# A fused attention and MLP kernel: another order of calls from the second batch on, and 27 scaled copies on VectorE in place of ScalarE

## The chip, the cores and the metric

The kernel runs on one core of a Trainium2 chip. The core has five engines that run their own instruction queues side by side: TensorE (PE in the profile; its weight loads are listed apart as PEld), VectorE (DVE), ScalarE (ACT), GpSimd (POOL) and SyncE (SP), and 16 DMA engines. The metric is the device time of one execution in microseconds; the median of three runs is taken.

## The reference

```python
def _attn_ref(q, k, v, g_q, g_k):          # (8, 12, 448, 64), float32
    def rmsnorm(x, g):
        return x / np.sqrt(np.mean(x * x, axis=-1, keepdims=True) + 1e-06) * g
    q_n, k_n = rmsnorm(q, g_q), rmsnorm(k, g_k)
    scores = 1.0 / np.sqrt(64) * np.matmul(q_n, k_n.transpose(0, 1, 3, 2))
    attn = np.exp(scores - np.max(scores, axis=-1, keepdims=True))
    attn = attn / (np.sum(attn, axis=-1, keepdims=True) + 1e-09)
    return np.matmul(attn, v)

# x: the attention's output as (3584, 768); w_in (768, 2048), w_out (2048, 768), alpha (2048,)
def _moe_ref(x, w_in, w_out, alpha):
    h = x @ w_in
    g = np.maximum(h, 0.0) + alpha * np.minimum(h, 0.0)
    return g @ w_out
```

Attention of 8 batches with 12 heads each, then an MLP with a PReLU between its two products over all 3584 tokens.

## The kernel before

The work of a batch is cut into three groups of four heads; a group has the number y = 3 x batch + i (i = 0, 1, 2), so y runs from 0 to 23. For a group, load_qk fetches q and k (SP's queue), square (L365, GpSimd) and reduce (L386, VectorE) and fold (L403, L406, VectorE) sum the squares, root (L416, L417, ScalarE) takes the inverse root, scale (L423, GpSimd) multiplies, flip or turn (L531, VectorE; or PE with a copy) transposes, and weigh (L541, ScalarE) puts the gains on k. score(y, j) (L588, PE) makes one of seven blocks of scores into a pair of PSUM banks, and soft(y, j) (L602, ScalarE) its exponentials. den and den_pre (L613, L637) sum them on PE, log and invert (L661, L671, ScalarE) make the reciprocal, attend (L613, PE) multiplies with v, and times (L709, VectorE) divides into xT, the MLP's input.

The MLP of a batch b runs over 16 blocks of 128 hidden columns. up(b, ft) (L726, PE, six matmuls of 128x128 by 448 columns) makes h in one PSUM bank, slope(b, ft) writes alpha x h to gT (L766 on ScalarE, L761 on VectorE), and larger(b, ft) (L772, VectorE) takes the larger of h and that; after larger the bank is free for PE. The second product is taken in tiles of 128 tokens by 384 columns: the first as down (L792, PE) with down_end (L803, VectorE, and a store on SP's queue, L778), and from tile 6 on by pairs of tiles with seven products in place of eight: mix_weights, mix_two and mix_rest (L822, L842, L843, L850, mostly GpSimd) form sums of weights and of gT, qa1 to qc2 (L854, PE) multiply them, and qa1v to qc2v (VectorE) add up and send. quad does a whole pair at the end.

PSUM has three pools: "sc", two pairs of banks for scores; "acc", one pair, for attend, den and whatever has its argument spare set to 1; and "mm", two banks for up, down, the q-products, den_pre and the second half of attend. A tile of a pool can be written again when the last reader of the tile that had its place is done. Other pools: q and k as loaded (nat) four places, scaled q and k (qs) three, results (osb) five.

The order of everything is written out by hand as a text, PLAN, of some 1330 calls, such as `up(5,8,1) qa1(14,0) soft(18,5)`. The loop at the end of the kernel makes the calls in that order; each call puts its instructions on the queues of its engines, so the text sets the order on each engine, and an engine never goes past an instruction that waits. Semaphores between engines follow from the tiles.

Of the kernel before, what the change touches and what calls it, by code (L numbers as in the profile page):

```python
# [24 lines left out]
opening() part_square(q,0:1,0:7,act) part_square(q,1:2,0:7,act) part_reduce(q,0:1,0:7) spin(2,0)  # L25
part_reduce(q,1:2,0:7) part_root(q,0:7) part_square(k,0:2,0:3,act) part_scale(q,0:7,7,pool)
part_reduce(k,0:2,0:3) part_square(k,0:2,3:7,act) square(1,q) load_w_in(1) spin(1)
part_reduce(k,0:2,3:7) part_root(k,3:7) reduce(1,q) square(1,k) part_root(k,0:3) gains()
part_turn(q,r0-7) load_qk(3) spin(1,0) part_scale(k,0:3,3,vec) part_turn(k,r0-3)
part_scale(k,3:7,4,vec) part_copy(q,0:7,vec) part_turn(k,r3-7) load_v(0) reduce(1,k) follow(0,k)  # L30
square(2,q) part_copy(k,0:3,vec) part_copy(k,3:7,vec) root(1) square(2,k) score(0,0,0) soft(0,0)
reduce(2,q,0) score(0,4,1) load_w_in(0) score(0,3,0) spin(1) reduce(2,q,1) soft(0,3) score(0,1,0)
scale(1,k) scale(1,q) soft(0,4) score(0,2,0) soft(0,2) reduce(2,k) score(0,6,1) turn_one(1,q)
soft(0,1) turn_one(1,k) score(1,0,1) score(1,3,0) spin(1) score(1,2,0) soft(0,6) root(2) soft(1,0)
load_qk(4) soft(1,3) scale(2,k) scale(2,q) follow(2,q) square(3,q) square(3,k) load_w_in(2)
soft(1,2) score(0,5,1) score(1,1,0) soft(0,5) soft(1,1) score(1,5,0) turn(2) soft(1,5) score(1,6,1)
# [9 lines left out]
slope(0,2) slope(0,3) larger(0,4) up(0,5,0) larger(0,2) larger(0,3) root(5) soft(3,6) slope(0,5)  # L46
soft(3,2) larger(0,5) up(0,6,0) scale(4,k) turn(4) scale(5,q) up(0,8,0) score(4,0,0) slope(0,6)
score(4,1,1) square(6,k) larger(0,6) slope(0,8) score(3,5,0) up(0,9,0) load_w_out(1) scale(5,k)
soft(4,0) square(7,q) larger(0,8) up(0,11,0) load_qk(8) score(4,2,0) score(3,3,0) soft(3,5)
load_v(1) square(7,k) up(0,7,1) soft(4,1) slope(0,9) up(0,10,0) reduce(6,q) square(8,q) reduce(6,k)  # L50
load_w_out(2) soft(4,2) up(0,12,0) slope(0,11) larger(0,9) soft(3,3) score(3,4,0) slope(0,10)
score(4,3,0) larger(0,11) larger(0,10) slope(0,7) larger(0,7) up(0,13,0) soft(3,4) slope(0,12)
larger(0,12) turn(5) up(0,14,0) square(8,k) soft(4,3) score(4,6,0) slope(0,13) score(4,4,1) root(6)
slope(0,14) larger(0,13) up(0,15,0) scale(6,q) reduce(8,q) soft(4,4) score(5,4,0) larger(0,14)
scale(6,k) score(5,0,1) reduce(7,q) slope(0,15) larger(0,15) down(1,0,0) score(5,2,1) score(4,5,0)
soft(4,6) soft(5,0) soft(5,4) soft(5,2) score(5,1,0) soft(4,5) down(0,0,0) turn(6) load_w_out(3)
den(3+4,1) reduce(7,k) attend(3+4,0,0) score(5,5,0) score(5,6,0) soft(5,1) mix_weights(0,1) log(3+4)
invert(3+4) soft(5,5) soft(5,6) mix_weights(0,3) attend(3+4,1,0) score(6,0,1) score(5,3,0) soft(6,0)
score(6,4,0) down_end(0,0) down(2,0,0) soft(5,3) root(7) scale(7,q) load_qk(9) soft(6,4) scale(7,k)
den(5,0) attend(5,0,1) down_end(1,0) mix_weights(0,2) times(3+4,0,0) times(3+4,1,0) times(3+4,1,1)  # L60
load_qk(10) log(5) down(0,1,0) reduce(8,k) invert(5) down_end(2,0) times(5,0,1) times(5,0,0)
times(5,0,3) times(5,0,2) score(6,5,1) mix_weights(0,0) score(6,1,0) down_end(0,1) score(6,6,0)
soft(6,5) turn(7) up(1,1,1) square(9,q) down(1,1,0) root(8) reduce(9,q) soft(6,6) score(6,3,1)
score(7,0,0) slope(1,1) score(6,2,0) up(1,2,0) up(1,0,0) soft(6,1) soft(7,0) soft(6,3) square(9,k)
up(1,3,1) up(1,4,0) slope(1,2) slope(1,0) larger(1,1) down_end(1,1) reduce(9,k) root(9) larger(1,2)
load_qk(11) larger(1,0) slope(1,3) scale(8,q) soft(6,2) up(1,7,0) slope(1,4) larger(1,3) larger(1,4)
scale(8,k) score(7,4,0) slope(1,7) larger(1,7) up(1,5,1) scale(9,q) turn(8) score(7,5,0) soft(7,4)
score(7,1,0) up(1,6,0) square(10,q) slope(1,5) larger(1,5) up(1,10,0) soft(7,5) soft(7,1) up(1,8,1)
scale(9,k) up(1,9,0) reduce(10,q) score(7,2,0) slope(1,6) slope(1,10) larger(1,6) mix_weights(1,1)
score(7,6,0) slope(1,8) slope(1,9) soft(7,6) up(1,12,1) up(1,11,0) soft(7,2) square(10,k) up(1,13,0)  # L70
larger(1,8) larger(1,10) slope(1,12) score(7,3,0) larger(1,9) up(1,14,1) slope(1,11) slope(1,13)
mix_weights(1,3) reduce(10,k) up(1,15,0) load_v(2) soft(7,3) larger(1,12) load_qk(12) score(8,3,0)
score(8,0,0) den(6+7,0) slope(1,14) fold(10) root(10) slope(1,15) soft(8,0) down(2,1,0) larger(1,11)
larger(1,13) square(11,q) log(6+7) score(8,1,0) score(8,4,0) soft(8,3) flip(9,k) scale(10,q)
larger(1,14) larger(1,15) score(8,5,1) mix_weights(3,1) down_end(2,1) reduce(11,q) square(11,k)
weigh(9) soft(8,5) down(3,0,0) soft(8,1) scale(10,k) score(8,2,0) flip(9,q) reduce(11,k)
score(8,6,0) soft(8,4) fold(11) load_qk(13) attend(6+7,0,0) attend(6+7,1,0) score(9,1,0)
score(9,0,0) down_end(3,0) soft(8,2) invert(6+7) score(9,2,1) down(3,1,0) times(6+7,0,0) soft(8,6)
root(11) times(6+7,1,0) load_qk(14) flip(10,q) down(4,0,1) mix_weights(1,2) soft(9,0) times(6+7,1,1)
score(9,5,0) square(12,q) soft(9,1) soft(9,2) scale(11,q) score(9,3,0) square(12,k) reduce(12,q)  # L80
down_end(3,1) soft(9,5) mix_weights(3,2) flip(10,k) scale(11,k) down_end(4,0) den_pre(8)
reduce(12,k) soft(9,3) attend(8,0,0) log_pre(8) score(9,6,0) fold(12) invert(8) root(12)
score(9,4,0) weigh(10) times(8,0,3) down(5,1,0) soft(9,4) times(8,0,1) times(8,0,0) flip(11,q)
down(4,1,0) score(10,0,0) soft(9,6) score(10,3,1) down_end(5,1) times(8,0,2) soft(10,0) soft(10,3)
score(10,2,0) up(2,0,0) up(2,1,0) slope(2,0) score(10,6,0) score(10,1,1) up(2,7,0) up(2,2,0)
down_end(4,1) up(2,4,1) slope(2,1) flip(11,k) soft(10,2) soft(10,1) slope(2,7) up(2,3,0)
mix_weights(2,0) slope(2,2) larger(2,0) scale(12,q) soft(10,6) slope(2,4) up(2,6,0) scale(12,k)
up(2,8,1) larger(2,1) slope(2,3) mix_weights(2,3) mix_weights(1,0) larger(2,7) square(13,k)
larger(2,2) up(2,10,0) square(13,q) up(2,5,0) larger(2,4) weigh(11) up(2,12,1) larger(2,3)
slope(2,6) up(2,14,0) slope(2,8) reduce(13,q) score(10,5,0) slope(2,10) mix_weights(2,2) load_v(3)  # L90
slope(2,5) slope(2,12) slope(2,14) score(10,4,0) soft(10,4) square(14,q) up(2,9,1) up(2,13,0)
soft(10,5) slope(2,13) larger(2,6) larger(2,8) larger(2,10) reduce(13,k) up(2,11,0) larger(2,5)
larger(2,12) load_qk(15) score(11,0,0) fold(13) den(9+10,1) slope(2,11) mix_weights(3,3) qa1(6,0)
up(2,15,0) qa2(6,1) root(13) mix_weights(3,0) flip(12,q) slope(2,9) larger(2,14) larger(2,13)
down(5,0,0) log(9+10) slope(2,15) larger(2,11) larger(2,9) invert(9+10) soft(11,0) square(14,k)
flip(12,k) reduce(14,q) weigh(12) qa1v(6) larger(2,15) mix_weights(2,1) scale(13,q) score(11,3,1)
scale(13,k) score(11,4,0) attend(9+10,0,1) mix_two(6,pool) soft(11,4) qa2v(6) mix_rest(6)
# [1000 lines left out]
```

## Time and profile before

| | us |
|---|---|
| median of three runs | 412.58 (412.21 to 413.02) |
| the profiled execution | 410.69 |
| its span, first to last instruction | 408.6 |
| busy in the span: PE | 395.3 |
| busy in the span: POOL | 299.9 |
| busy in the span: ACT | 270.4 |
| busy in the span: DVE | 268.3 |

A profile line of a group names the line of the code, the engine, the operation, what is written from what, how often, and after the bar the busy time, the mean of one in ns, and the idle time of the engine just before with what ended it. A timeline line has the start, the length, the engine, the line, the operation, the count of instructions drawn together, and in brackets the idle time before and who ended it. The ends of matmuls are modelled, so the length of a group of matmuls overlaps the next one's; starts are the better measure of pace.

### The profile page before, as it was taken

To read this page: it belongs to the slowest core of one execution; us is meant where nothing else is said; L and a number is where in the kernel's file an instruction comes from. 1 tells how busy PE (TensorE), PEld (TensorE's weight loads), DVE (VectorE), ACT (ScalarE), POOL (GpSimd) and SP (SyncE) were. 2 spreads that over 40 slices of the span, in tenths; PEclk is the share of its full clock that TensorE was granted. 3 is DMA by queue.
4 is the path that set the end of the run, shared out by engine and by line. 5 is a ranking of instruction groups with operands and counts; after the bars stand their busy time and mean duration, and the time that the engine had idled before them with its cause. 6 is when DMAs were issued, how large, how long until landed. Compare 5 with 4: busy or idle time off the path is not lost.

```text
span 408.6 us, 11992 instructions
## 1 busy us (share of the span) xinstructions
PE 395.3 (97%) x5083; PEld 210.3 (51%) x5083; DVE 268.3 (66%) x480; ACT 270.4 (66%) x405; POOL 299.9 (73%) x200
## 2 busy tenths in 40 slices
PE   7688999999999999999999999999999999999996
PEld 3344445555455445554455455555555455655664
DVE  3957874676766685779678678886668545654422
ACT  5597686757885876767886987686876874245110
POOL 7977998497796998997796995589496809600780
PEclk9999999999999999999999999999999999999999
DMA  7999699796776794579952595794516000230143
GB/s 260 242 280 227 110 265 165 173 239 177 125 180 154 173 203 108 119 172 185 232 130 83 136 240 145 147 217 102 140 38 131 21 2 22 59 79 0 39 98 98
DMA packets 37222, 58.39 MB, mean 143 GB/s; under 512 B 4769, under 2 KB 28977, under 8 KB 37169
## 3 DMA queue, kind: packets, MB, share of 16 engines
q1 hardware_dynamic: 23232, 45.43, 43.2%
q0 software_dynamic: 13536, 11.81, 19.1%
q8 instruction: 39, 0.64, 0.7%
q10 hardware_dynamic: 400, 0.39, 0.3%
q14 instruction: 15, 0.11, 0.1%
HBM read 58.40 MB, written 11.01 MB: 170 GB/s over the span
## 4 chain that ended last, share of the span: by engine, by line
PE 88%; DVE 4%; DMA 3%; POOL 3%; issue 1%; POOLq 0%; DVEq 0%
PE hT L726 25%; PE hTa L726 9%; PE sc L588 8%; PE op L792 7%; PE qx L854 5%; PE av L613 5%; PE qz L854 4%; PE qc L854 4%; PE oq L854 4%; PE qxa L854 3%; PE avb L613 2%; PE dn L613 2%; PE oqm L854 2%; DMA w_in_sb<-in_moe_w_in_dram 2%; POOL nat L376 2%; DMA arena<-in_g_k_dram 2%
## 5 line engine op out<-in xcount | busy, mean ns | idle before, releaser
L602 ACT ACTIVATE expT<-sc 128x896 f16<-128x896 f32 x168 | 146.3, 916 | 40.9 <-PE sc L588 39.2
L726 PE MATMUL hT<-xT,w_in_sb 128*128 128x448 f16 x558 | 115.9, 353 | 1.6 <-DVE xT L709 1.4
L726 PEld LDWEIGHTS <-w_in_sb 128*128 128x128 f16 x768 | 73.0, 98 | 74.5 <-issue 9.9
L423 POOL TENSOR_TENSOR qs<-nat,rr 128x896 f16<-128x896 f32 x30 | 65.7, 2221 | 26.5 <-ACT rr L417 23.4
L766 ACT ACTIVATE gT<-hT,cols 128x448 f16<-128x448 f32 x92 | 58.4, 636 | 40.0 <-PE hT L726 38.9
L772 DVE TENSOR_TENSOR gT<-hT,gT 128x448 f16<-128x448 f32 x93 | 57.3, 619 | 38.2 <-ACT gT L766 37.5
L365 POOL TENSOR_TENSOR nat<-nat 128x896 f32<-128x896 f32 x30 | 50.7, 1697 | 8.1 <-DMA nat<-in_q_dram 7.7
L588 PE MATMUL sc<-qT,kT 64*32 64x448 f16 (+1 forms) x1092 | 49.4, 355 | 4.3 <-ACT expT L602 1.7
L854 PEld LDWEIGHTS <-gT 128*128 128x128 f16 x352 | 33.4, 98 | 25.5 <-issue 4.1
L726 PE MATMUL hTa<-xT,w_in_sb 128*128 128x448 f16 x198 | 42.9, 353 | 0.0
L842 POOL TENSOR_TENSOR gs<-gT 128x1024 f16<-128x1024 f16 x4 | 8.5, 2127 | 36.7 <-DVE gT L772 36.7
L709 DVE TENSOR_TENSOR xT<-av,rden 64x448 f16<-64x448 f32 (+1 forms) x37 | 27.2, 736 | 10.7 <-ACT rden L671 4.6
L386 DVE TENSOR_REDUCE sp<-nat 128x28 f32<-128x896 f32 x30 | 32.1, 1070 | 2.1 <-POOL nat L365 2.0
L588 PEld LDWEIGHTS <-kT 64*32 64x32 f16 (+1 forms) x1092 | 16.7, 93 | 32.4 <-issue 23.0
L792 PE MATMUL op<-w_out_sb,gT 128*128 128x384 f16 x176 | 30.3, 326 | 0.2 <-DVE xT L709 0.2
L766 ACT ACTIVATE gT<-hTa,cols 128x448 f16<-128x448 f32 x33 | 21.0, 636 | 10.5 <-PE hTa L726 10.0
L772 DVE TENSOR_TENSOR gT<-hTa,gT 128x448 f16<-128x448 f32 x33 | 20.4, 618 | 10.6 <-ACT gT L766 10.2
L613 PEld LDWEIGHTS <-vt 64*32 64x32 f16 x1344 | 19.7, 92 | 12.2 <-issue 1.9
L792 PEld LDWEIGHTS <-gT 128*128 128x128 f16 x192 | 18.3, 98 | 14.5 <-issue 3.0
L613 PE MATMUL av<-expT,vt 64*32 64x448 f16 x896 | 24.3, 350 | 0.0
L850 POOL TENSOR_TENSOR gT<-gT 128x1024 f16<-128x1024 f16 x11 | 23.5, 2133 | 0.0
L854 PEld LDWEIGHTS <-arena 128*128 128x128 f16 x136 | 12.6, 98 | 10.5 <-issue 2.3
(151 smaller groups left out, 572.5 us busy)
## 6 DMA issues: line engine op xcount, KB each, us to landing
nat<-in_q_dram SPq DMA_DIRECT2D x60, 216.0 KB, 4.1
nat<-in_k_dram SPq DMA_DIRECT2D x60, 216.0 KB, 5.0
out_dram<-osb SPq DMA_DIRECT2D x107, 96.0 KB, 3.1
vt<-in_v_dram POOLq DMA_DIRECT2D x8, 672.0 KB, 7.8
w_in_sb<-in_moe_w_in_dram POOLq DMA_DIRECT2D x24, 128.0 KB, 7.3
w_out_sb<-in_moe_w_out_dram POOLq DMA_DIRECT2D x4, 768.0 KB, 8.6
nat<-in_k_dram SPq DMA_DIRECT2D x6, 448.0 KB, 7.8
nat<-in_q_dram SPq DMA_DIRECT2D x5, 448.0 KB, 6.7
```

Source lines behind the costliest of these rows:

```text
L365: nc.gpsimd.tensor_mul(out=sqs[y, nm], in0=t[:, :, :HD], in1=t[:, :, :HD])
L386: nc.vector.tensor_reduce(out=parts[y][:, ts("qk".index(nm), 4 * J), :1], in_=sqs[y, nm], axis=AXIS_X, op=ALU.add,)
L423: nc.gpsimd.tensor_mul(out=t.rearrange("p j d n -> p n j d"), in0=nat[y, nm][:, :, :HD].rearrange("p (n j) d -> p n j d", j=J), in1=r.unsq ...
L588: nc.tensor.matmul(out=sc[ds(64 * g + m * c, m), par, :S].rearrange("p (j c) -> p j c", j=J), lhsT=kT[ds(64 * par, 64), j, g, ts(c, m)], r ...
L602: nc.scalar.activation(out=expT[y][:, j], in_=scs[y, j][:, :, :S], func=AF.Exp, scale=QK_SCALE, bias=EXP_BIAS,)
L613: nc.tensor.matmul(out=accs[g][ds(32 * n, 32), :S], lhsT=weights(g, y, par, c, j), rhs=expT[y][ds(64 * g, 64), j, par, :], start=(j == 0), ...
L709: nc.vector.tensor_mul(out=o, in0=p, in1=q)
L726: nc.tensor.matmul(out=hT[:, :S], lhsT=w_in_sb[:, block_of(g, i), ts(ft, 128)], rhs=xT[b][:, g, i, :], start=(i == 0 and g == 0), stop=(i ...
L766: nc.scalar.activation(out=g, in_=hT[:, :S], func=AF.Copy, scale=alpha_sb[:, ft : ft + 1])
L772: nc.vector.tensor_max(out=g, in0=hT[:, :S], in1=g)
L792: nc.tensor.matmul(out=op[:, :OH], lhsT=gT[:, ft, ts(tile % J, 128)], rhs=w_out_sb[:, ft, ts(oh, OH)], start=(ft == 0), stop=(ft == NF - 1),)
L854: nc.tensor.matmul(out=bank[:, c], lhsT=g[:, ft], rhs=v[:, ft, c], start=(first and ft == 0), stop=(ft == HF - 1), skip_group_check=True,)
```

## The change

The text PLAN is the same, call by call and engine by engine, up to `scale(8,q)`; from there on its calls come in another order, in nearly every line to the end. 27 more calls of slope are marked vec, which puts them on VectorE: (1; 4, 6, 7, 10, 13), (2; 0, 2, 4, 11), (3; 0, 7, 12), (4; 5, 9, 10, 12, 14), (5; 0, 2, 6, 7, 9), (6; 15) and (7; 1, 6, 8, 13), batch first. Which work takes a bank of "acc" changes in a number of calls. The number of instructions of PE (10149 with weight loads and others), POOL (205) and SP (250) stays; ACT has 412 to 385 and DVE 482 to 509.

```diff
-    def slope(b, ft):
+    def slope(b, ft, eng=None):
         hT, g = raised[b, ft]
-        if b == 0 and ft in (2, 3, NF - 4):
+        if eng is nc.vector:
             nc.vector.tensor_scalar(
                 out=g, in0=hT[:, :S], scalar1=alpha_sb[:, ft : ft + 1], scalar2=None,
                 op0=ALU.mult,
             )
         else:
             nc.scalar.activation(
                 out=g, in_=hT[:, :S], func=AF.Copy, scale=alpha_sb[:, ft : ft + 1]
             )
...
-    def load_w_in(c):
+    def load_w_in(c, lo, hi):
...
-    def square(y, nm):
+    def square(y, nm, eng=None, n=1):
...
     def soft(y, j):
-        if j == 0:
+        if y not in expT:
...
-        spin(2)
-        spin(17, False)
+    def factors():
```

load_w_in now takes which of its pieces to load, square which engine and in how many parts, and factors holds the last lines of opening; in the new text they are called so that the instructions of the first part are the same ones in the same order.

Of the text, the places that are spoken of below, in the order of the calls (before, then after). The calls from up(4,0) to the up after up(4,9):

```
up(4,0,0) root(18) larger(4,4) slope(4,7) up(4,3,1) up(4,5,0) score(16,6,0) soft(16,4) scale(17,k)
up(4,6,0) soft(16,1) soft(16,5) flip(17,q) slope(4,0) slope(4,3) larger(4,1) slope(4,5) soft(16,6)
larger(4,7) slope(4,6) mix_two(12,pool) larger(4,0) up(4,8,1) up(4,9,0) flip(17,k) scale(18,q)
weigh(17) slope(4,8) up(4,11,0)
```

```
up(4,0,0) up(4,3,1) soft(16,4) qc1v(10) soft(16,1) larger(4,2) slope(4,0) scale(17,q) soft(16,5)
up(4,5,0) mix_two(12,pool) larger(4,4) scale(17,k) up(4,6,0) flip(17,k) larger(4,1) flip(17,q)
slope(4,3) larger(4,7) larger(4,0) weigh(17) load_qk(20) up(4,8,1) up(4,9,0) scale(18,k) up(4,11,0)
larger(4,3) slope(4,5,vec) slope(4,6) slope(4,8) score(16,6,1) score(17,4,0) larger(4,5)
square(19,q) larger(4,6) soft(16,6) square(19,k) reduce(19,q) den(15+16,1) larger(4,8) scale(18,q)
slope(4,9,vec) reduce(19,k) score(17,5,1) larger(4,9) flip(18,k) slope(4,11) soft(17,5) larger(4,11)
up(4,10,0)
```

The calls from up(5,2) on:

```
up(5,2,0) weigh(19) score(18,4,0) slope(5,1) qc1v(12) score(18,5,1) load_qk(22) score(19,0,0)
up(5,5,0) larger(5,0) reduce(21,q) slope(5,3) larger(5,1) slope(5,2) larger(5,3) up(5,7,1) up(5,4,0)
up(5,6,0) up(5,8,1) qa1(14,0) soft(18,5) reduce(21,k) qa2(14,0) larger(5,2) soft(19,0) slope(5,5)
slope(5,7) slope(5,4) mix_two(14,pool) fold(21) up(5,9,0) root(21) larger(5,5) up(5,11,0)
score(19,2,0) larger(5,7) slope(5,6) larger(5,4) slope(5,8) score(19,1,1) larger(5,6) soft(18,4)
square(22,q) slope(5,9) flip(20,k) score(19,6,0) qa3(14,0) larger(5,8) slope(5,11) soft(19,6)
weigh(20) qa1v(14) mix_rest(14) flip(20,q) qa2v(14) larger(5,9) qb1(14,0) soft(19,2) up(5,13,0)
```

```
up(5,2,0) score(18,4,0) slope(5,0,vec) score(19,0,0) larger(5,0) soft(18,6) load_v(6) score(18,5,1)
slope(5,3) up(5,5,0) larger(5,1) up(5,7,1) up(5,4,0) up(5,6,0) up(5,8,1) qa1(14,0) soft(18,5)
square(21,k) score(19,6,0) score(19,1,1) slope(5,5) larger(5,3) score(19,2,0) qa2(14,0)
slope(5,2,vec) load_qk(22) larger(5,2) mix_two(14,pool) soft(18,4) slope(5,4) reduce(21,k) up(5,9,0)
fold(21) larger(5,5) scale(20,k) up(5,11,0) slope(5,7,vec) up(5,13,1) soft(19,0) larger(5,7)
slope(5,8) root(21) qa3(14,0) mix_rest(14) up(5,10,0)
```

The calls behind attend of heads 15 and 16:

```
attend(15+16,0,1) attend(15+16,1,0) slope(4,13) larger(4,8) larger(4,9) larger(4,11) log(15+16)
reduce(19,k) invert(15+16) larger(4,10) larger(4,12) fold(19) score(17,2,1) score(17,3,0) qa1v(12)
score(17,1,0) larger(4,13) root(19) qa2v(12) reduce(20,q) up(4,15,0) qa3v(12) weigh(18) soft(17,5)
soft(17,2) soft(17,3) flip(18,q) times(15+16,0,0) qb1(12,1) times(15+16,1,0) scale(19,q) slope(4,15)
square(20,k) soft(17,1) up(4,14,0)
```

```
attend(15+16,0,1) slope(4,13) reduce(20,q) soft(17,4) score(17,6,1) larger(4,13) scale(19,k)
qa1v(12) qa2v(12) soft(17,3) flip(18,q) reduce(20,k) qa3v(12) scale(19,q) score(18,0,0) qb1(12,0)
times(15+16,1,1) score(17,2,1) score(17,0,0) soft(17,1) fold(20) score(18,1,0) times(15+16,0,0)
times(15+16,1,0) qb1v(12) flip(19,q) flip(19,k) soft(17,6) soft(18,0) up(4,14,0)
```

More of the change, by code (lines that the diff above doesn't have):

```diff
@@ L24 @@
 PLAN = """
[L25 to L36, printed above, removed]
@@ L45 @@
 larger(0,0) score(3,2,0) score(3,6,0) slope(0,1) load_qk(7) follow(2,k) larger(0,1) slope(0,4)
[L46 to L97, printed above, removed]
@@ new lines @@
+down_end(2,0) times(5,0,1) times(5,0,0) times(5,0,3) times(5,0,2) score(6,5,1) mix_weights(0,0)
+score(6,1,0) down_end(0,1) score(6,6,0) soft(6,5) turn(7) up(1,1,1) square(9,q) down(1,1,0) root(8)
+reduce(9,q) soft(6,6) score(6,3,1) score(7,0,0) slope(1,1) score(6,2,0) up(1,2,0) up(1,0,0)
+soft(6,1) soft(7,0) soft(6,3) square(9,k) up(1,3,1) up(1,4,0) slope(1,2) slope(1,0) larger(1,1)
+down_end(1,1) reduce(9,k) root(9) larger(1,2) load_qk(11) larger(1,0) slope(1,3) scale(8,q)
+scale(8,k) score(7,4,0) up(1,7,0) larger(1,3) mix_weights(1,3) scale(9,k) slope(1,4,vec)
@@ new lines @@
+scale(13,q) larger(2,13) invert(9+10) reduce(14,q) fold(14) score(11,1,0) mix_two(6,pool) qa2v(6)
+attend(9+10,0,0) attend(9+10,1,0) down_end(5,0) score(11,2,0) soft(11,1) score(12,0,0) qa3(6,1)
+times(9+10,0,0) soft(11,0) qb1(6,0) soft(12,0) score(11,6,1) times(9+10,1,1) soft(11,2)
+score(11,5,0) score(12,1,0) mix_rest(6) root(14) qb2(6,0) qc1(6,1) times(9+10,1,0) qa3v(6)
+score(12,3,0) qb1v(6) soft(11,6) flip(13,k) soft(11,5) qb2v(6) soft(12,1) den_pre(11) attend(11,0,1)
+soft(12,3) qc1v(6) square(15,q) log_pre(11) score(12,6,0) invert(11) mix_two(8,pool) score(12,2,1)
@@ new lines @@
+load_qk(16) soft(12,2) qa1(8,0) qa2(8,1) times(11,0,3) weigh(13) flip(13,q) times(11,0,0) soft(12,6)
+qc2(6,0) qa3(8,0) qa1v(8) reduce(15,q) scale(14,q) times(11,0,1) score(13,0,0) times(11,0,2)
+score(12,5,1) qa2v(8) scale(14,k) score(13,6,0) mix_rest(8) qc2v(6) soft(12,5) qa3v(8) up(3,0,0)
+qb1(8,0) score(12,4,0) slope(3,0,vec) square(15,k) load_qk(17) score(13,3,0) soft(13,6) qb2(8,1)
+qb1v(8) larger(3,0) reduce(15,k) up(3,2,0) soft(13,0) soft(12,4) up(3,4,0) qb2v(8) up(3,1,1)
+fold(15) soft(13,3) square(16,q) slope(3,2) up(3,8,0) up(3,3,0) up(3,5,1) score(13,2,0) slope(3,4)
@@ new lines @@
+root(21) qa3(14,0) mix_rest(14) up(5,10,0) score(19,4,0) larger(5,4) score(19,3,0) soft(19,1)
+score(19,5,1) square(22,k) slope(5,6,vec) qb1(14,0) larger(5,6) larger(5,8) qa1v(14) soft(19,6)
+scale(21,k) load_qk(23) soft(19,2) qb2(14,0) flip(20,q) square(22,q) up(5,14,1) qa2v(14)
+slope(5,9,vec) slope(5,11) up(5,15,0) scale(21,q) slope(5,13) slope(5,10) larger(5,9) reduce(22,k)
+larger(5,11) qa3v(14) soft(19,5) larger(5,13) flip(20,k) soft(19,4) up(5,12,0) weigh(20)
+larger(5,10) reduce(22,q) soft(19,3) slope(5,14) fold(22) qb1v(14) slope(5,15) qb2v(14)
@@ new lines @@
+soft(22,4) den(21+22,1) slope(6,13) attend(21+22,0,1) larger(6,10) larger(6,12) slope(6,14)
+score(23,2,0) mix_rest(18) score(23,5,1) soft(23,0) qb1(18,0) qa2(18,1) qa3(18,0) qa1v(18)
+log(21+22) qa1(20,1) score(23,3,0) soft(23,5) larger(6,13) larger(6,14) slope(6,15,vec) larger(6,15)
+invert(21+22) attend(21+22,1,0) qa2v(18) score(23,1,0) mix_two(20,pool,nat) soft(23,2) score(23,4,0)
+mix_rest(20) times(21+22,0,0) qa3v(18) soft(23,3) qb1v(18) mix_two(22,pool,expT) qb2(18,1) qa2(20,0)
+qa1v(20) times(21+22,1,0) score(23,6,0) soft(23,4) times(21+22,1,1) soft(23,1) soft(23,6)
@@ L1034 @@
     acts = dict(
+        factors=factors,
         attend=attend, begin=begin, den=den, den_pre=den_pre, down=down, down_end=down_end,
```

273 lines of the change are left out of this document (156 added, 117 removed).

## The prediction

> **What bounds the kernel now.** I read the busy shares of the page first, then the stretches of the span, then PE's own timeline in places. The page:
>
> ```profile
> span 408.6 us, 11992 instructions
> ...
> PE 395.3 (97%) x5083; PEld 210.3 (51%) x5083; DVE 268.3 (66%) x480; ACT 270.4 (66%) x405; POOL 299.9 (73%) x200
> ...
> L602 ACT ACTIVATE expT<-sc 128x896 f16<-128x896 f32 x168 | 146.3, 916 | 40.9 <-PE sc L588 39.2
> ...
> L766 ACT ACTIVATE gT<-hT,cols 128x448 f16<-128x448 f32 x92 | 58.4, 636 | 40.0 <-PE hT L726 38.9
> L772 DVE TENSOR_TENSOR gT<-hT,gT 128x448 f16<-128x448 f32 x93 | 57.3, 619 | 38.2 <-ACT gT L766 37.5
> ```
>
> PE is busy for 97% of the span. ScalarE and VectorE, between which the change moves work, are busy for 66% each. The stretches (a row: start and length, then busy us and count of PE, PEld, DVE, ACT and POOL, then the granted clock, DMA share, GB/s) say where PE's 3% are:
>
> ```profile
> 97.00:226.00 129.00, 128.82 (x1846) 67.90 (x1844) 93.59 (x177) 96.03 (x141) 109.72 (x62) 1.00 0.70 159
> 226.00:310.00 84.00, 83.82 (x1212) 44.50 (x1205) 61.11 (x117) 65.65 (x96) 66.13 (x37) 1.00 0.62 140
> 310.00:377.00 67.00, 67.00 (x725) 35.64 (x723) 37.77 (x68) 35.73 (x54) 28.30 (x14) 1.00 0.21 46
> 377.00:408.60 31.60, 27.74 (x186) 17.54 (x184) 10.37 (x20) 3.92 (x8) 16.86 (x8) 1.00 0.30 76
> ```
>
> The two orders of calls are the same up to the call scale(8,q), which in the trace lies at about 97 us; nothing before that can change. From 97 to 377 us PE shows 0.18 + 0.18 + 0.00 = 0.36 us without work, and after 377 us it works 27.74 us without a hole, then the last copies and stores follow. So the kernel is bound by the sum of PE's work, and a different order can win only these 0.36 us, what the order itself costs PE, and stalls hidden in the modelled ends of matmuls.
>
> **What the order itself costs PE.** PE's own timeline from 148 us:
>
> ```profile
> 148.16 1.30 PE L726 MATMUL hTa<-xT,w_in_sb 128*128 128x448 f16 x6
> 149.30 1.30 PE L726 MATMUL hT<-xT,w_in_sb 128*128 128x448 f16 x6
> 150.52 0.57 PE L588 MATMUL sc<-qT,kT 64*32 64x448 f16 x16
> 151.03 1.31 PE L726 MATMUL hTa<-xT,w_in_sb 128*128 128x448 f16 x6
> 152.18 2.43 PE L726 MATMUL hT<-xT,w_in_sb 128*128 128x448 f16 x12
> 154.54 0.38 PE L588 MATMUL sc<-qT,kT 64*32 64x448 f16 x8
> 154.74 1.51 PE L613 MATMUL dn<-expT,ones 64*32 64x448 f16 x56
> ```
>
> From start to start an up that an up follows takes 149.30 - 148.16 = 1.14 us, one that a score follows 150.52 - 149.30 = 1.22. A score followed by other 64-row work takes 154.74 - 154.54 = 0.20; two scores followed by an up take 151.03 - 150.52 = 0.51, so the last of them 0.31. Each excursion from 128-row to 64-row matmuls and back costs 0.08 + 0.11, about 0.2 us. Counting them in the two orders from scale(8,q) on gives 46 before and 44 after. **Term 1: 2 x 0.2 = -0.4 us.** PE's instructions are otherwise the same in number and shape.
>
> **The stalls that go or stay.** Both stretches' idle time stands before one call each:
>
> ```profile
> 122.03 0.48 PE L792 MATMUL op<-w_out_sb,gT 128*128 128x384 f16 x2 [0.17 <-DVE xT L709]
> ```
>
> ```profile
> 121.35 0.62 DVE L709 TENSOR_TENSOR xT<-avb,rden 128x448 f16<-128x448 f32 x1
> ```
>
> ```profile
> 252.35 0.62 DVE L709 TENSOR_TENSOR xT<-avb,rden 128x448 f16<-128x448 f32 x1 [0.15 <-PE avb L613]
> ```
>
> ```profile
> 253.03 0.54 PE L726 MATMUL hT<-xT,w_in_sb 128*128 128x448 f16 x2 [0.18 <-DVE xT L709]
> ```
>
> down(3,1) waits for times of heads 6+7, up(4,15) for times of 15+16: three scores lie between, 0.69 us, too little for a 0.62 us product that starts late. In the new order down(3,1) again follows attend(6+7) and three scores, so its stall stays. After attend(15+16) come two scores, then qb1(12,0), which needs nothing of these heads: that stall goes. **Term 2: -0.2 us.**
>
> **The scaled copies.** The diff marks 27 more slopes for VectorE. Their prices:
>
> ```profile
> L761 DVE TENSOR_SCALAR gT<-hTb,cols x2: 674/679/684, 44.5 to 45.1; 128x448 f16<-128x448 f32 x2
> ```
>
> ```profile
> 44.95 1.70 POOL L436 TENSOR_TENSOR qs<-nat,rr 128x896 f16<-128x896 f32 x1
> ```
>
> ```profile
> L436 POOL TENSOR_TENSOR qs<-nat,rr x6: 1684/1688/1702, 45.0 to 79.8; 128x896 f16<-128x896 f32 x6
> ```
>
> ScalarE is relieved of 27 x 0.636 = 17.2 us, VectorE takes 27 x 0.679 = 18.3. By batch: 12 in batches 1 to 3 (97 to 226 us), 10 in batches 4 and 5 (226 to 310), 5 in 6 and 7. VectorE then stands at 93.6 + 8.1 = 101.7 of 129 us in the first stretch and at 61.1 + 6.8 = 67.9 of 84 in the second, still below PE. On average they are hidden under PE and cost nothing; with no cover each costs its 0.68 us. A slope and its larger on one engine spare one hand-over, but a slope on VectorE also stands in front of every larger behind it, and a larger is what gives a PSUM bank back to PE. So the price lies where PE is about to need that bank.
>
> As to the shared port, the second of those slopes starts at 45.1 us, inside the GpSimd product of 44.95 us, which took 1.70 us against 1.684 to 1.702 for all six: not lengthened. The Trainium skill (SBUF — State Buffer, Who interferes with whom) lists tensor_scalar among the operations that can take the port pair shared with GpSimd, whoever issues first blocking the other, but exempts one with at most one SBUF input outside the 2-port modes. The input here is PSUM, and the row agrees with the exemption; by the blocking half of the rule the sum would be that of rival C.
>
> **New waits.** Rows of the fourth-to-sixth batch stretch of before, for durations:
>
> ```profile
> 268.53 0.76 PE L588 MATMUL sc<-qT,kT 64*32 64x448 f16 x24
> 269.22 1.31 PE L726 MATMUL hT<-xT,w_in_sb 128*128 128x448 f16 x6
> 270.37 1.30 PE L726 MATMUL hTa<-xT,w_in_sb 128*128 128x448 f16 x6
> 271.50 2.43 PE L726 MATMUL hT<-xT,w_in_sb 128*128 128x448 f16 x12
> ```
>
> ```profile
> 268.71 1.08 DVE L386 TENSOR_REDUCE sp<-nat 128x28 f32<-128x896 f32 x1
> 269.70 0.62 DVE L772 TENSOR_TENSOR gT<-hT,gT 128x448 f16<-128x448 f32 x1
> 270.35 0.85 DVE L403 TENSOR_REDUCE sp<-sp 32x56 f32<-32x56 f32 x4
> 271.23 0.27 DVE L406 TENSOR_REDUCE ss<-sp 128x56 f32<-128x112 f32 x1
> 271.45 0.62 DVE L772 TENSOR_TENSOR gT<-hT,gT 128x448 f16<-128x448 f32 x1
> ```
>
> Three scores take 269.22 - 268.53 = 0.69 us, an up (271.50 - 269.22) / 2 = 1.14, from start to start a reduce 269.70 - 268.71 = 0.99 and a fold 271.45 - 270.35 = 1.10.
>
> At up(5,8), whose bank larger(5,7) gives back: VectorE's new order from the end of up(5,2) is slope(5,2), larger(5,2), reduce(21,k), fold(21), larger(5,5), slope(5,7), larger(5,7): 0.68 + 0.62 + 0.99 + 1.10 + 0.62 + 0.68 + 0.62 = 5.31 us. PE in that time has the three scores and up(5,5), (5,7), (5,4), (5,6): 0.69 + 4 x 1.14 = 5.25. With two hand-overs of 0.05 (the product of 252.35 ends at 252.97 and its matmul starts at 253.03) PE waits 0.2. Queued behind on PE are up(5,8) and all after it, so the wait moves the end. Before, slope(5,7) ran on ScalarE beside VectorE's work.
>
> At up(4,9), whose bank larger(4,5) gives back: from the start of up(4,0), ScalarE has soft(16,4), soft(16,1), slope(4,0), soft(16,5), slope(4,3), 3 x 0.92 + 2 x 0.64 = 4.04; then VectorE larger(4,3), slope(4,5), larger(4,5), 0.62 + 0.68 + 0.62 = 1.92: 5.96. PE has five ups, 5.70. With three hand-overs the wait is 0.4.
>
> Walked in the same way, turn(8), up(2,12), up(3,1) and qa3(12) come out 0.03 to 0.16 late, 0.36 together; that is the error of such a walk, and I take half, 0.2. **Term 3: +0.2 + 0.4 + 0.2 = +0.8 us**, between 0 (each chain finds its queue 0.4 us earlier) and 2.2 (the bound of rival B).
>
> **Moved loads and GpSimd.** The nearest hand-over of GpSimd to PE is the mixing ahead of qa3(6):
>
> ```profile
> 160.20 2.13 POOL L842 TENSOR_TENSOR arena<-gT 128x1024 f16<-128x1024 f16 x1 [0.16 <-DVE gT L772]
> 162.40 2.13 POOL L843 TENSOR_TENSOR arena<-arena,gT 128x1024 f16<-128x1024 f16 x1
> ```
>
> ```profile
> 166.34 1.48 PE L854 MATMUL qxa<-arena 128*128 128x384 f16 x8
> ```
>
> It ends at 164.53, 1.8 us before qa3 starts. In the new order the same two products follow scale(13,k) and scale(13,q), and qa3(6) comes 0.6 us earlier on PE, so over 1 us is left: 0. SP's queue gets load_qk(15) ahead of the store of down_end(4,1); that store's buffer is wanted by qb1v(6), some 3 us later by my walk: 0, and what it overruns if the cover is gone. The other edits (factors apart from opening, load_w_in by pieces, soft making its tile at the first call) give the same instructions in the first 97 us: 0.
>
> **Sum.** -0.4 - 0.2 + 0.8 = +0.2 us. It is made against the profiled execution: 410.69 us, its span of 408.6 and 2.1 around it. That is 1.9 us below the median of the runs, 412.58; I put the difference on the median: **412.8 us.** A measurement of this kernel can tell about 0.2% (0.83 us) from no change, so this is "within". Own range: terms 1 and 2 alone give 412.0, term 3 at double 413.6.
>
> **The rivals.**
>
> A, faster: the saved excursions stay and every new hand-over holds, both stalls of the rows go. -0.4 - 0.36 = -0.8; the modelled ends can hide as much again (-1.2), so 411.4 to 411.8. For it: ScalarE is 17 us freer, so softs and slopes start earlier than my durations' chains assume. Against: the two walks above need no late start to overrun. 0.22.
>
> B, slower: VectorE's queue becomes the bound of the batch 4 and 5 stretch. Ten slopes of 0.68 us each stand there ahead of larger calls; it decides from the point at which VectorE's backlog at a bank's release exceeds what PE still has in its other banks, two ups or 2.3 us. Price: between none and all of 10 x 0.68 = 6.8; the up(5,8) and up(4,9) chains are already at the edge, and one in three reaching it gives 2.2. 412.6 - 0.6 + 2.2 = 414.2. Against: 67.9 of 84 us on average. 0.29.
>
> C, slower: a VectorE slope blocks GpSimd. Nine slopes of batches 1 and 2 lie ahead of the mixing for qa3(6): 9 x 0.68 = 6.1, less its 1.8 margin: 4.3 at most, half of it where GpSimd idles between: 2.1. 412.8 + 2.1 = 414.9. Against: the 1.70 us row. 0.03. The skill's rule on the shared pair named above is this mechanism.
>
> D, the change does nothing to PE's sum beyond swapping one stall for another is the forecast, 0.44. The remaining 0.02 go to something late in the last 30 us.
>
> **How the numbers follow.** The likeliest is the forecast, 412.8. The range runs from 411.5, inside rival A, to 414.4, just over B; A's lowest end, B's dearer half and C lie outside. Faster by over 0.2% needs nearly all of A: 0.22. Slower is B, C and the rest: 0.34. Within: 0.44.
>
> **What would show it.** Right: PE without a hole but for some tenths before up(4,9) and up(5,6) or up(5,8), released by VectorE's larger; no wait before up(4,15); VectorE's slope rows at 0.67 to 0.69 us; GpSimd's rows unchanged. Wrong: the two stretches of PE with 0.1 us idle or less (A); over 1.5 us of PE idle released by larger between 226 and 310 us (B); GpSimd products that overlap a slope longer than 2.13 or 2.22 us (C); or a difference before 97 us, which the order excludes.

## The result and the profile after

The changed kernel takes 415.00 us (median of 20 runs, 412.47 to 416.49), the kernel before 412.09 (20 runs, 410.25 to 414.98): ratio 1.0067, 95% interval 1.0048 to 1.0086. It is slower by 2.8 us by the ratio (2.9 between the medians), where 0.2 was forecast and 414.4 was the top of the range. The profiled execution took 415.17 us with a span of 413.2.

The page of after, the lines that answer to those shown of before:

```profile
span 413.2 us, 11978 instructions
...
PE 398.0 (96%) x5083; PEld 211.2 (51%) x5083; DVE 286.1 (69%) x507; ACT 255.3 (62%) x378; POOL 299.1 (72%) x200
...
L770 ACT ACTIVATE gT<-hT,cols 128x448 f16<-128x448 f32 x69 | 43.7, 633 | 36.9 <-PE hT L729 36.3
```

VectorE has 17.8 us more to do and ScalarE 15.1 less, close to the 18.3 and 17.2 of the prediction. PE is still the bound. Two views of after follow: first the stretches that the prediction showed of before, cut at the same times, then the same execution cut at the first matmul of up(1,1) (which starts at 85.40 us before and at 87.54 after) and behind the last matmul:

```profile
97.00:226.00 129.00, 128.25 (x1807) 67.49 (x1804) 98.34 (x184) 89.79 (x129) 107.56 (x61) 1.00 0.67 153
226.00:310.00 84.00, 83.44 (x1191) 43.79 (x1197) 67.79 (x127) 57.88 (x84) 64.94 (x35) 1.00 0.64 146
310.00:377.00 67.00, 67.00 (x783) 35.92 (x767) 41.48 (x76) 35.58 (x52) 31.45 (x16) 1.00 0.23 50
```

```profile
0.00:87.54 87.54, 77.57 (x1054) 39.43 (x1055) 58.34 (x86) 60.25 (x94) 69.49 (x78) 0.98 0.97 211
87.54:409.40 321.86, 320.47 (x4033) 171.78 (x4030) 227.47 (x422) 195.02 (x284) 229.66 (x123) 1.00 0.54 123
```

PE's idle time from 97 to 377 us is 0.75 + 0.56 = 1.3 us, where it was 0.36. And the execution was already 2.14 us behind at up(1,1), ahead of the first changed instruction. From here on two numbers are told for each kernel: the start of up(1,1), and **the way**, from that start to the start of the last group of 16 matmuls in the tail. Before, the way is 403.25 - 85.40 = 317.86 us, after 407.82 - 87.54 = 320.29; the difference is 2.43.

Where the way is lost shows in PE's starts, call by call, against the paces that the prediction read from before (an up 1.14 us, a score 0.20, and so on). The table lists by how many us a call started later than that pace; the first two columns are the two profiles of after (the second is the run after_again below):

```
call that starts late    after  again   what it waited for, by the program's waits
score(9,4) in attend(8)   0.83   0.65   nothing (see below); down(4,1) behind it 0.16
score(15,4)               0.52   0.52   qc2v(10), on VectorE behind reduce(18,q)
up(2,12)                  0.27   0.27   larger(2,8), on VectorE behind fold(13)
up(5,6), up(5,8)          0.36   0.36   larger(5,5), slope(5,7), larger(5,7) behind reduce and fold(21)
up(5,1), (5,3), (5,2)     0.23   0.23   larger(5,0) behind slope(5,0) behind qc1v(12)
attend(18+19)             0.22   0.23   soft(20,3), on ScalarE behind root(22)
score(12,5)               0.20   0.20   qa2v(8), on VectorE behind two times
score(9,2)                0.18   0.18   soft(8,5), on ScalarE behind root(11)
up(4,15)                  gone   gone   (0.24 before)
down(3,1)                 0.07   0.07   (0.24 before)
```

The rows in which the two largest are seen, on PE's own timeline and VectorE's:

```profile
129.85 0.86 PE L640 MATMUL dnb<-expT,ones 64*32 64x224 f16 x56
130.52 1.50 PE L616 MATMUL av<-expT,vt 64*32 64x448 f16 x53
132.67 0.37 PE L616 MATMUL av<-expT,vt 64*32 64x448 f16 x3 [0.64 <-issue]
132.68 0.73 PE L591 MATMUL sc<-qT,kT 64*32 64x448 f16 x16
```

```profile
227.87 1.07 DVE L387 TENSOR_REDUCE sp<-nat 128x28 f32<-128x896 f32 x1
...
228.87 0.55 DVE L930 TENSOR_TENSOR osb<-qca,osb 128x384 f32<-128x384 f32 x1
...
229.47 0.76 PE L591 MATMUL sc<-qT,kT 64*32 64x448 f16 x24 [0.44 <-DVE osb L930]
```

The second is a plain place in a queue: qc2v(10) (L930) gives back the "acc" bank that score(15,4) writes, and a reduce of 1.07 us was put ahead of it. The first is another thing: PE stops three matmuls before the end of attend(8), and what the profile names is "issue", PE itself. From here on this stop is called the hole. The row's 0.64 us counts from the modelled end of the matmul before; from start to start the gap is 0.99, which the table has as 0.83 at score(9,4) and 0.16 at down(4,1).

### The profile page after: what moved, and what is told of

Read it like the earlier page. It is cut to its first block, busy times and chain, and to the rows that moved or that the text cites. A ratio compares the mean times of both kernels' runs of the same rounds, so it can differ in the third digit from the quotient of the medians.

```text
span 413.2 us, 11978 instructions
## 1 busy us (share of the span) xinstructions
PE 398.0 (96%) x5083; PEld 211.2 (51%) x5083; DVE 286.1 (69%) x507; ACT 255.3 (62%) x378; POOL 299.1 (72%) x200
## 5 line engine op out<-in xcount | busy, mean ns | idle before, releaser
L729 PE MATMUL hT<-xT,w_in_sb 128*128 128x448 f16 x564 | 117.5, 353 | 1.8 <-DVE xT L712 1.6
L424 POOL TENSOR_TENSOR qs<-nat,rr 128x896 f16<-128x896 f32 x30 | 65.5, 2215 | 28.1 <-ACT rr L418 16.6
L776 DVE TENSOR_TENSOR gT<-hT,gT 128x448 f16<-128x448 f32 x94 | 57.7, 619 | 21.7 <-ACT gT L770 20.7
L770 ACT ACTIVATE gT<-hT,cols 128x448 f16<-128x448 f32 x69 | 43.7, 633 | 36.9 <-PE hT L729 36.3
L729 PE MATMUL hTa<-xT,w_in_sb 128*128 128x448 f16 x192 | 41.5, 352 | 0.1
L770 ACT ACTIVATE gT<-hTa,cols 128x448 f16<-128x448 f32 x29 | 18.4, 635 | 20.7 <-PE hTa L729 20.4
L846 POOL TENSOR_TENSOR gs<-gT 128x1024 f16<-128x1024 f16 x4 | 8.5, 2126 | 29.8 <-DVE gT L776 29.8
L776 DVE TENSOR_TENSOR gT<-hTa,gT 128x448 f16<-128x448 f32 x32 | 19.9, 620 | 9.1 <-ACT gT L770 8.7
L796 PEld LDWEIGHTS <-gT 128*128 128x128 f16 x192 | 18.3, 98 | 14.2 <-issue 2.5
L854 POOL TENSOR_TENSOR gT<-gT 128x1024 f16<-128x1024 f16 x11 | 23.4, 2130 | 0.0
L765 DVE TENSOR_SCALAR gT<-hT,cols 128x448 f16<-128x448 f32 x25 | 16.9, 677 | 2.5 <-PE hT L729 2.2
```

Source lines behind the costliest of these rows:

```text
L424: nc.gpsimd.tensor_mul(out=t.rearrange("p j d n -> p n j d"), in0=nat[y, nm][:, :, :HD].rearrange("p (n j) d -> p n j d", j=J), in1=r.unsq ...
L729: nc.tensor.matmul(out=hT[:, :S], lhsT=w_in_sb[:, block_of(g, i), ts(ft, 128)], rhs=xT[b][:, g, i, :], start=(i == 0 and g == 0), stop=(i ...
L770: nc.scalar.activation(out=g, in_=hT[:, :S], func=AF.Copy, scale=alpha_sb[:, ft : ft + 1])
L776: nc.vector.tensor_max(out=g, in0=hT[:, :S], in1=g)
L796: nc.tensor.matmul(out=op[:, :OH], lhsT=gT[:, ft, ts(tile % J, 128)], rhs=w_out_sb[:, ft, ts(oh, OH)], start=(ft == 0), stop=(ft == NF - 1),)
```

## The experiments

In the diffs a line is one call of the order of calls, and the rest is the kernel named.

**Is the opening chance?** Before and after once more, unchanged.

> The kernel before, unchanged, profiled a second time. PE's start of up(1,1) lies at 85.40 us in the first profile of before and at 87.54 in that of after, though the instructions up to there are the same; from there to the last 16 matmuls of the tail PE takes 317.85 us before and 320.28 after. Theory 1, the 2.14 us ahead of up(1,1) are chance of single executions (the first loads, the granted clock): this run starts up(1,1) anywhere between 85 and 88 us, and the way from there is again 317.85 within 0.3. Theory 2, the 2.14 us belong to the changed program: 85.4 within 0.3 here, 87.5 in the repeat of after.

> The changed kernel, unchanged, profiled a second time. Theory 1 (chance): up(1,1) starts between 85 and 88 us, not tied to 87.5. Theory 2 (the program): 87.5 within 0.3. For both the way from up(1,1) to the last 16 matmuls is 320.28 us within 0.3, apart from the 0.8 us hole inside attend(8) at 132 us, which the profile puts on PE's own issue: if that is chance too, the way is 319.5.

up(1,1) started at 87.78 us in this profile of before and at 85.86 in that of after, the other way round than the first time; over all 14 profiles of the study, whose instructions up to there are the same, it lies between 84.75 and 87.78. The ways were 317.89 and 320.12. So the opening is chance, of up to 3 us, and the way is the measure: after loses 2.2 to 2.4 us on it, and the hole in attend(8) is in both profiles of after and not a chance of one.

**The slopes alone, the order alone.** slopes_only has before's order, with each of the 27 slopes taken out of ScalarE's queue and put right ahead of its larger; order_only has after's order with the 27 on ScalarE.

```diff
-slope(5,7)
...
+slope(5,7,vec)
 larger(5,7)
```

> Before's order with the same 27 slopes on VectorE, each directly ahead of its larger; nothing else differs. Theory 1, the slopes on VectorE hold up the calls that free PSUM banks (rival B of the prediction): most of the 2.43 us that after loses behind up(1,1) appears here, a way of 319.5 us or more from up(1,1) to the last 16 matmuls, with PE waits released by larger. Theory 2, the cost lies in the searched places of the other calls: 317.8 to 318.4 us.

> After's order with the 27 slopes back on ScalarE, each put among ScalarE's calls by the place of its up on PE. Theory 1 (slopes cost): the way from up(1,1) falls to 318.4 us or below, near before's 317.85. Theory 2 (places cost): it stays at 319.5 or above, with the 0.52 us wait ahead of score(15,4) and the 0.2 us waits ahead of score(9,2), score(12,5) and attend(18+19) still there.

slopes_only: way 319.95, ratio 1.0044 (1.0019 to 1.0070), theory 1. Before's order pays 2.1 us for the slopes on VectorE, and the profile names larger (L776) as the one that PE waits for. PE's waits from 97 us on (waiting, for whom, total us, times, longest):

```profile
PE hT L729 <- DVE gT L776: 0.5, 2, 0.3
PE dn L616 <- DVE gT L776: 0.4, 1, 0.4
PE dnb L640 <- DVE gT L776: 0.2, 1, 0.2
```

One of them is the wait that I had forecast for after at up(4,9), 0.44 us here and none there. order_only: way 328.41, ratio 1.0226 (1.0192 to 1.0261), theory 2, with waits of PE up to 1.7 us for larger and a hole of 2.0 in attend(8). The waits of after ahead of score(15,4), score(9,2), score(12,5) and attend(18+19) are in it with the same 0.2 to 0.5 us, so these do not come from the slopes. The two parts can't be added: the changed order counts on the slopes being on VectorE, and my places for them on ScalarE follow a plain rule (the place of the up), which costs PE waits that neither kernel has. Alone, either is slower than before.

**Four mendings of after.**

```diff
 down(3,1,0)
+score(9,3,0)
+score(9,5,0)
 down(4,0,1)
-score(9,3,0)
-score(9,5,0)
 den_pre(8)
```

> After, with score(9,3) and score(9,5) put ahead of down(4,0) on PE. After stops 0.83 and 0.65 us (two profiles) before the last 3 matmuls of attend(8), for no wait that the program holds there; some 110 pairs of matmul and weight load, all of them 64-row, lie between PE's last instruction load (129.8 us) and the hole. Theory 1, PE has used up its instructions before the next 16 KB of them arrive: with the slow 16 matmuls of down(4,0) among those pairs the hole is gone or under 0.1 us, and the way from up(1,1) to the last 16 matmuls falls from 320.2 (mean of both profiles) to 319.6, one more excursion (0.2) counted. Theory 2, something that attend(8) reads is late (v, exponentials, the reciprocal's bank): the hole stays at 0.6 or more, 320.4.

Way 321.15, worse than either theory said. The hole stayed (0.89), and a new one of 0.58 opened in front of down(4,0), at PE's matmul number 1499. By this run alone theory 2 was ahead; the table of instruction blocks below shows why it is not: the block ahead of the hole began later here than in after, at matmul 1539 in place of 1515, so the slower matmuls won nothing. The new hole lies one block, 125 matmuls, ahead of the old one, and belongs to that block's own transfer: PE goes on at 126.71, 1.6 us after its end (125.10).

```diff
+qc2v(10)
 reduce(18,q)
...
+larger(2,8)
 fold(13)
...
+qa2v(8)
 reduce(15,q)
...
+soft(8,5)
 root(11)
...
+soft(20,3)
 root(22)
```

> After, with five calls moved ahead of one or two others in the queues of VectorE and ScalarE: qc2v(10) ahead of reduce(18,q), larger(2,8) ahead of fold(13), qa2v(8) ahead of reduce(15,q), soft(8,5) ahead of root(11), soft(20,3) ahead of root(22). Theory 1, the waits of PE behind these calls are their place in the queue and nothing else: 0.52 ahead of score(15,4), 0.27 ahead of up(2,12), 0.20 ahead of score(12,5), 0.18 ahead of score(9,2) and 0.22 ahead of attend(18+19) go to 0.05 or less, and the way falls by 1.2 to 1.4, from 320.2 to about 318.9. Theory 2, each wait only moves to the next call, since VectorE is full in these stretches (rival B): the way stays above 319.6 and PE waits for the calls that were put behind.

Way 320.74, but with a hole of 1.90 us in attend(8); without the hole 318.84, where after without it is 319.47. So 0.6 to 0.7 us came back, half of theory 1's 1.3. All five waits went; score(15,4) now starts on time:

```profile
227.05 0.76 PE L592 MATMUL sc<-qT,kT 64*32 64x448 f16 x24
227.74 1.31 PE L730 MATMUL hT<-xT,w_in_sb 128*128 128x448 f16 x6
```

Others took the place of some: up(3,0) 0.29, up(4,1) 0.18, down(3,1) 0.24 again, score(20,1) 0.12. Both theories were half right.

```diff
-slope(5,0,vec)
...
-slope(5,7,vec)
+slope(5,0)
 slope(5,1)
...
+slope(5,7)
 slope(5,4)
```

> After, with slope(5,0) and slope(5,7) back on ScalarE. Theory 1, VectorE's slopes cost only where they stand ahead of a larger that PE waits for: the waits of 0.12 ahead of up(5,2) and 0.11 ahead of up(5,8) go, the 0.24 ahead of up(5,6) stays (it waits for larger(5,5) behind reduce and fold): way 319.9 to 320.1. Theory 2, ScalarE is the fuller engine there and softs get late: 320.2 or more.

Way 319.55 with a hole of 0.25, so 319.30 without it against 319.47: the waits at up(5,2) and up(5,8) went, 0.06 came back at up(5,6). Theory 1.

> After with all the edits of the three kernels beside it, and larger(5,5) ahead of fold(21). If the cost of the changed order is these single places, their waits add up: way 320.2 - 0.5 (fetch, one excursion counted) - 1.3 (queues) - 0.5 (slopes and larger(5,5)) = 317.9, the 317.87 of before, and a ratio to before between 0.997 and 1.003. If the waits only move on, the way stays above 319 and the ratio above 1.003.

All the edits together gave a way of 319.89 (ratio 1.0029, 0.9995 to 1.0063), 1.1 us of it still in the two holes near attend(8) and down(4,0). That is far from the 317.9 of the sum; without the holes it is 318.8, since up(3,0), up(4,1) and qa3(12) now came 0.2 to 0.3 late. That hole had to be understood first.

**The hole.** In all 14 profiles a DMA queue called "instruction" (q8 on the page: 39 or 40 transfers, 0.64 to 0.66 MB) brings blocks of 16 KB. I take it for PE's: the program has 10149 PE instructions, which in as many blocks makes about 256 to a block, or up to 128 pairs of weight load and matmul, and fx_fetch's two holes lie 125 matmuls apart. Beside each other, for the profiles: PE's matmul number at which the last block but one and the last block ahead of the hole began to be transferred, the end of that transfer, the time of the 54th matmul of attend(8) (number 1624), and how long the 54th came after the 53rd:

```
run             block 1 at   block 2 at   its end   54th at   gap
before            1411         1496        127.92    129.53   0.00
before_again      1419         1497        130.51    131.99   0.07
slopes_only       1435         1497        128.02    129.65   0.00
after             1473         1515        131.15    132.67   0.99
after_again       1475         1523        129.46    130.81   0.81
order_only        1475         1601        131.87    133.35   2.20
fx_fetch          1474         1539        130.96    132.34   1.04
fx_queue          1474         1595        129.35    130.89   2.06
fx_slope          1474         1507        128.44    129.78   0.41
fx_all            1473         1515        129.40    130.73   0.77
spread_10         1451         1512        128.53    129.92   0.71
bunch_10          1478         1579        130.30    131.53   1.49
fx_all2           1467         1495        128.24    130.01   0.00
fx_all2_again     1467         1539        130.65    132.02   1.05
```

In every run with a gap above 0.1, the 54th matmul comes 1.2 to 1.5 us after the end of block 2's transfer, whatever the gap. Number 1624 is 128 beyond 1496, where in the undisturbed runs the block begins to be transferred: PE seems to ask for a block when it enters the one before. In before the time from 1496 to 1624 is 2.8 us, nearly all of it 64-row matmuls, and a transfer of 1.1 to 1.4 us with the 1.2 to 1.5 behind it takes nearly as long. What keeps the block waiting is then soon a hole. It is block 2 that counts for this hole: fx_all2 has block 1 late and block 2 on time, and no gap. In time it is plainer: counted from the start of matmul 1496, block 2 began 0.94 us later in after, where the gap is 0.99, 0.66 in fx_slope (0.41) and 2.22 in order_only (2.20); in all eight profiles with a gap above 0.1 and no second hole the two agree within 0.3 us, and in the four without a gap it began between 0.29 us earlier and 0.14 later.

What differs ahead of it is in SP's queue. GpSimd's scale gives back the buffer that the next load of q or k takes, and the changed order put scale(10,k) and scale(10,q) one behind the other. GpSimd, then SP, of after:

```profile
113.67 4.24 POOL L424 TENSOR_TENSOR qs<-nat,rr 128x896 f16<-128x896 f32 x2
```

```profile
115.91 1.72 SPq L324 DMA_DIRECT2D nat<-in_q_dram  x4
117.94 1.72 SPq L324 DMA_DIRECT2D nat<-in_k_dram  x4
119.76 2.67 SPq L782 DMA_DIRECT2D out_dram<-osb  x4
125.93 1.73 SPq L324 DMA_DIRECT2D nat<-in_q_dram  x4
```

and SP of before, where a piece of mix_weights and a square lie between the two scales:

```profile
112.25 1.72 SPq L321 DMA_DIRECT2D nat<-in_q_dram  x4
117.53 1.73 SPq L321 DMA_DIRECT2D nat<-in_k_dram  x4
119.36 1.11 SPq L778 DMA_DIRECT2D out_dram<-osb  x2
123.68 1.74 SPq L321 DMA_DIRECT2D nat<-in_q_dram  x4
```

The last columns of the windows view (granted clock, DMA share, GB/s; a share of 1.00 is all 16 engines busy), after first, then before, show the DMA engines full from 118 to 124 us in the one and not in the other:

```profile
118.00:121.00 3.00, 3.00 (x45) 1.54 (x51) 0.83 (x3) 2.97 (x4) 1.37 (x1) 1.00 1.01 225
121.00:124.00 3.00, 3.00 (x128) 1.55 (x112) 2.91 (x8) 1.68 (x4) 1.94 (x2) 1.00 1.03 227
```

```profile
118.00:121.00 3.00, 3.00 (x121) 1.70 (x128) 2.15 (x6) 2.62 (x4) 2.59 (x2) 1.00 0.85 198
121.00:124.00 3.00, 2.83 (x53) 1.56 (x38) 2.91 (x5) 2.59 (x5) 2.22 (x1) 1.00 0.65 168
```

This is the time in which block 1 waits. Counted from the start of matmul 1368, 128 ahead of 1496, it began 1.1 to 1.6 us later in the three profiles with before's order on GpSimd, and 3.7 to 4.5 us later in the eight with the two scales together. Why block 2 was late in after these rows do not show: its DMA share was 1.02 while block 2 waited (128.88 to 129.82 us), but in before it was 1.00 as well (126.74 to 127.92), where block 2 went at once, and the load of q ahead of it was issued 3.0 and 3.1 us before matmul 1496.

Two runs put the loads to the test, one in each direction.

```diff
 fold(10)
+root(10)
+scale(10,k)
 square(11,k)
...
-root(10)
-scale(10,k)
```

> After, with GpSimd's two products scale(10,k) and scale(10,q) taken apart again (square(11,k) between them, root(10) a little earlier), so that the two loads of group 12 that wait for them are issued some 4 us apart in place of 2. In six profiles of the changed order the hole in attend(8) ends 1.33 to 1.54 us after the end of an instruction load of PE that began late; the one before it began at PE's matmul 1473 in place of 1411 to 1435 as in before's order, while the DMA engines were full from 116 to 125 us. Theory 1, the loads of group 12, bunched, hold up PE's instruction load: it starts at matmul 1450 or earlier and the hole in attend(8) falls below 0.2 us, way 319.4 to 319.7. Theory 2, the hole comes from the density of 64-row matmuls alone: it stays between 0.25 and 2.1 us.

```diff
-scale(10,q)
...
+mix_weights(1,2)
+scale(10,q)
 scale(10,k)
...
-mix_weights(1,2)
```

> Before's order on ScalarE, VectorE and PE, with scale(10,q) put right ahead of scale(10,k) on GpSimd (mix_weights(1,2) ahead of both), as after has them: the reverse of the run beside it. Theory 1 (bunched loads delay PE's instructions): the instruction load that began at matmul 1411 to 1435 begins at 1450 or later, and a hole of 0.2 us or more opens in attend(8), in a kernel that had 0.00 to 0.07 there; way 318.1 to 319. Theory 2 (density alone, or the searched order elsewhere): no hole, 317.8 to 318.0.

bunch_10 is clear, as far as one execution can be: before's order with the two scales together opens a hole that the three profiles with before's order on GpSimd do not have, and its way goes from 317.9 to 319.31, a little above what theory 1 said. PE's timeline there:

```profile
128.88 1.50 PE L615 MATMUL av<-expT,vt 64*32 64x448 f16 x53
131.53 0.37 PE L615 MATMUL av<-expT,vt 64*32 64x448 f16 x3 [1.14 <-issue]
```

against before, in one piece:

```profile
128.38 1.51 PE L613 MATMUL av<-expT,vt 64*32 64x448 f16 x56
129.70 0.56 PE L588 MATMUL sc<-qT,kT 64*32 64x448 f16 x16
```

Block 1 began at number 1478 in place of 1411, block 2 at 1579 in place of 1496. spread_10 is a miss in part: block 1 came earlier (1451 in place of 1473 to 1475), but a hole of 0.55 stayed (way 320.04). SP then issued the loads of the next group at 122.4 and 126.0, and block 2 may have met the second of them; that is not shown, since fx_all2 below has them at 123.3 and 127.0 and no hole. Shown are two things: a late block 2 is the hole, and bunched loads hold up block 1 by 2 to 3 us. That they can hold up block 2 rests on bunch_10; that they are all that does so in after is not shown.

**The mended order.**

> After with the five queue moves, the two slopes back on ScalarE, larger(5,5) ahead of fold(21), the spread loads of group 12, and for the waits that the queue moves gave back reduce(15,q) behind qa3v(8) and qc1v(10) ahead of fold(18). If single places are the whole cost: from 320.2 less 0.7 (hole), 1.1 (queues), 0.25 (slopes), 0.25 (larger(5,5)): a way of 317.9, within 0.3 of before's 317.87, and a ratio to before between 0.996 and 1.004. If VectorE as a whole is too full (rival B): above 318.6.

> The mended order of the run before (fx_all2), unchanged, again: its way was 317.70 us against 317.86 and 317.89 of before, without a hole in attend(8). If the mending is real, the way is 317.7 within 0.3 again and the hole under 0.2; if the missing hole was chance, the hole is 0.25 to 2 us and the way 318 to 319.7. Either way the ratio to before lies between 0.996 and 1.004, since the ways differ by 0.05%.

First a way of 317.70, ratio 1.0003 (0.9972 to 1.0034), no hole and 0.16 to 0.19 us below before's; then 318.76, ratio 1.0006 (0.9987 to 1.0024), with a hole of 0.89. Without holes both ways are 317.7 to 317.9. The waits of the table are thus what after loses, the hole aside. 25 of the 27 slopes are still on VectorE in this kernel, so VectorE as a whole is not too full (rival B). The mended order is no better than before by its times, and the hole comes and goes between two executions of it.

## Why the prediction was wrong

**The bound, and term 1 (excursions, -0.4), held.** PE stays the bound to the end, and the paces that gave term 1 reproduce after's way with the waits in the table.

**Term 2 (stalls that go, -0.2) held in sum.** The wait ahead of up(4,15) went; that of down(3,1), said to stay, shrank by 0.17, but only because 0.18 stands ahead of score(9,2) just before it.

**Term 3 (new waits, +0.8) is the step that failed, by its size.** The kind was right: larger, and what hands banks back, late on VectorE. up(5,6) and up(5,8), 0.2 forecast, were 0.36; up(2,12), one of four walks of 0.03 to 0.16, was 0.27, and the other three were on time. up(4,9), 0.4 forecast, was nothing: my chain took three softs and two slopes at their lengths, 0.92 and 0.64 us, and they follow one another faster, a soft at 0.80 to 0.81 from start to start (soft(16,4) at 235.64, soft(16,1) at 236.45) and a slope at 0.51 (237.25 to 237.76), so larger(4,5) ended at 241.12, just in time for PE at 241.18. What was not walked at all cost most: score(15,4) 0.52, up(5,1) to up(5,2) 0.23, attend(18+19) 0.22, score(12,5) 0.20, score(9,2) 0.18. Two of these five were on ScalarE, which I had counted as relieved. In sum the queue waits were about 2.0 us in place of 0.8.

**Moved loads at nothing was wrong too.** I followed one hand-over of GpSimd (the mixing ahead of qa3(6)), which did hold, and one store, and not that two loads now came together. The hole was worth 0.65 to 0.83 us, and 0.16 behind it. It comes from PE's own instruction blocks, which I had not looked at; that the bunched loads alone make it in after stays open. 2.0 + 0.9 + some 0.3 of smaller waits - 0.8 for what went (0.24 and 0.17 of the two stalls, 0.4 of term 1) is 2.4, where the ways say 2.2 to 2.4. The median's 2.9 agrees with it within its interval (0.5 to 0.9% of 412 is 2.0 to 3.5 us).

**The rivals.** A fell. B's price of 2.2 us came true in slopes_only to a tenth (2.1), in part by luck: 0.8 of that, ahead of den(6+7) and up(3,13), lies outside the stretch that B named. In after the two slopes that were put back cost 0.2 (fx_slope), and the mended order carries the other 25 without loss; B named the right sign and not the cause. C fell: GpSimd's products of L424, L846 and L854 took 2.215, 2.126 and 2.130 us in the mean, where they had taken 2.221, 2.127 and 2.133, with 27 more VectorE slopes of 0.675 us beside them; the nine of these products that overlap a slope took 2.20 to 2.22 (L424) and 2.13 to 2.14 (L854). The Trainium skill's exemption (SBUF — State Buffer, Who interferes with whom) agrees.

The range ended at 414.4 since its top was B alone; several small waits, each below 0.6 us, together with the hole went past it.

## What to carry to other kernels

Where one engine is busy for over 99% of a stretch, as PE is here from 97 to 377 us, a new order has to be followed at every hand-over to it, not at the places that look crowded: five of the waits stood where a misplaced reduce, fold, root or times was to blame, and all five went when it was moved. Lateness along a queue is summed from start to start, since lengths overlap by a tenth of a microsecond (a soft is 0.92 long, and the next starts 0.81 behind it). And a pair of loads that moves together can change everything that uses the DMA engines, the instructions of the busiest engine among them.
